# A planned instruction order for attention with a gated feed-forward block: planned again with four other times, and a last value product over 128 rows

## The chip, the cores and the metric

The kernel runs on one core of one Trainium2 chip. The metric is the device time of one execution in microseconds, the median of three runs. Beside it stands one execution that the hardware profiler recorded, with its own time; all rows of the profile come from that one.

## What is computed

Two branches on 2,048 tokens of width 512, mixed by a gate per token. The first is attention with 32 heads of 16 columns, the second a feed-forward block of width 1,376 whose hidden values are the product of two projections:

```python
g = sigmoid((x * gate_w).sum(-1))
q, k, v = split(x @ wqkv)              # 32 heads, 16 columns each
p = softmax(q @ k.T * 16 ** -0.5)
a = (p @ v) @ wo
b = ((x @ w_gate) * (x @ w_up)) @ w_down
out = g * a + (1 - g) * b
```

The feed-forward block is fed the same x. All inputs and the output are bf16.

## The kernel before, in words

**Tiles.** The tokens of the queries go in four chunks (c) of 512. A step is one of 32 groups of four heads for one chunk (a "quad", `quad`) and 128 keys (kt): four score blocks of 128 keys by 512 queries, one per head, then their exponentials, then the value products that add into bank 7 of PSUM. A matmul uses 64 rows and 32 columns of TensorE (PE), an eighth of it. Four matmuls side by side in the columns make a *job* (`pe64`, L1721); a job belongs to one of two row halves, r = 0 or 1, and both halves run jobs at the same time. Two score jobs of the same keys in a row share their weights, and the second leaves the weight load out (`keep`).

**Two ways for an exponential.** Steps of kind A go to ScalarE (ACT, `exp`, L1840). Steps of kind D go to VectorE (DVE, `dpass`, L1873), which makes a rough exponential by integer arithmetic; three more versions with other offsets are made by DVE or GpSimd (POOL, `copy`, L1879 and L1880), and all four are multiplied with the values. So a D step has eight value jobs, an A step two, one per half.

**Fill units.** Projections, the feed-forward products and the output products are units of 8 to 30 jobs (`_Unit`). They start strictly in the order of one list, `self.fill`, by `f_start` (L664): only the unit at its head may start, and only if what it reads is there.

**The planner.** No order is written out. `_Sched` (L138) simulates the engines event by event when the program is built, with a duration for every kind of instruction, and each decision appends an instruction to its engine's list. `_Plan.emit` then puts the lists out with semaphores for the true dependences. The chip follows the lists in order on each engine, and starts an instruction as soon as its semaphores allow; the planner's times are in no instruction. What decides between ready jobs are about 45 tables in `PAR` (limits of score blocks in flight, priorities, pairings). A table holds one entry per 2.0 us (`win`) of the planner's clock, written as (count, value) runs and read by `g` (L178); beyond its end the last entry is used. Before the change each table has 322 entries.

**Times that the planner assumes**, and that the change touches:

- `ilat`, in `take` (L262): instructions of PE come in packets of 256; a packet asked for near the end of the one before is taken to be there `ilat` later.
- `wgap`, in `weights` (L501), `late` (L507) and `wd_go` (L532): spacing of the weight loads on SP's queue. `weights` issues 36 loads: four pieces of w_up, four of w_gate, and so on in turn, then four of wo; a load is taken to land 3.0 us after its issue.
- `tx`, in `prologue` (L1508): when the four chunks of x, transposed by DMA (issued at L2048), are there.
- `mmarg`, in `norm2` (L1270): how long after the broadcast of the softmax denominators' reciprocals (rb, 256 KB, L2030) landed the multiplication of a normalized group is put on DVE (`mult`, L2038). POOL's copies wait for the last such multiplication.

**The end.** The last value product of quad 31 leads to `tail_norm` (L1986 to L1992: shuffle, product, logarithm and exponential for the reciprocal, product), and then to `tail_out` (L2001 to L2018): one more product of 128 rows for each of four output tiles, the sums with the feed-forward part, and the stores. The output products of the last chunk ("fin" units) run at the same time as the last value products.

`v_job` (L416) emits a value job and `pv` (L1771) its matmuls. A change of half in bank 7 waits for the last job of the other half.

Of the kernel before, what the change touches and what calls it, by code (L numbers as in the profile page):

```python
# [137 lines left out]
class _Sched:  # L138
# [277 lines left out]
    def v_job(self, r):  # L416
# [1141 lines left out]
    def run(self):  # L1558
# [22 lines left out]
        self.vcount = [0] * NG  # L1581
        self.vh = 0
# [72 lines left out]
class _Hw:  # L1655
# [385 lines left out]
    def prologue(self):  # L2041
# [114 lines left out]
        if self.par["acc"]:  # L2156
# [23 lines left out]
 'alook': ((3, 2), (1, 1), (5, 2), (16, 1), (2, 6), (25, 2), (4, 6), (1, 5), (1, 2), (2, 6), (9, 2), (1, 4), (1, 5),  # L2180
# [12 lines left out]
 'amax': ((4, 5), (5, 4), (3, 5), (1, 4), (4, 5), (2, 4), (2, 6), (1, 5), (2, 6), (21, 4), (1, 6), (6, 4), (5, 3),  # L2193
# [3 lines left out]
 'amin': ((3, 4), (1, 2), (12, 4), (1, 3), (4, 4), (1, 3), (5, 4), (10, 2), (1, 4), (1, 2), (6, 4), (1, 3), (4, 4),  # L2197
# [5 lines left out]
 'apick': ((16, 1), (3, 0), (3, 1), (5, 0), (3, 1), (5, 0), (4, 1), (3, 0), (3, 1), (1, 0), (4, 1), (2, 0), (5, 1),  # L2203
# [4 lines left out]
 'ares': ((7, 2), (2, 1), (4, 0), (8, 1), (1, 2), (16, 1), (1, 0), (1, 1), (5, 0), (2, 1), (3, 0), (2, 2), (3, 1),  # L2208
# [6 lines left out]
 'await': ((1, 0.1), (3, 0), (3, 0.2), (2, 0.05), (3, 0), (4, 0.05), (13, 0), (9, 0.05), (1, 0.1), (8, 0.05), (5, 0),  # L2215
# [168 lines left out]
 'lg': [3, 4],  # L2384
 'mga': 0.0,
 'mgd': 0.0,
 'mmarg': 0.6,
 'ndum': 6,
 'npre': 0,
 'olead': 2.2,  # L2390
# [145 lines left out]
```

## Time and profile before

| what | value |
|---|---|
| median of three runs | 654.78 us (654.52 to 656.81) |
| the profiled execution | 654.76 us |
| its span, first to last instruction | 653.0 us |
| matmuls, weight loads | 22,841 and 18,026 |
| granted clock of TensorE | 0.999 |

In rows by time, the first number is the start in us, the second the length; "x4" means four instructions merged. In rows of a group, three durations are the shortest, median and longest in ns, then come the first and last start. In rows of waits, the numbers are us in total, times, and (where there are three) the longest. In rows of a stretch, each engine's busy time stands with its count of instructions in brackets: PE, weight loads (PEld), DVE, ACT, POOL, then the granted clock, the share of the DMA engines and GB/s.

### The profile page before, as it was taken

The numbers are of one execution on the slowest core, as the hardware profiler recorded it, in microseconds if no ns is written. First come the engines' busy times: TensorE is split into PE (matmuls) and PEld (weight loads), VectorE is DVE, ScalarE is ACT, GpSimd is POOL, SyncE is SP. The second block draws the span as 40 slices with busy tenths as digits, with TensorE's granted clock in tenths as the row PEclk, the third lists the DMA queues.
The fourth block names the chain that finished last, engine by engine and source line by source line (L and its number), as shares of the span: only waits on it lengthen the run. The fifth ranks groups of instructions, "written<-read, shape, count | busy, mean of one in ns | idle before, by whom it ended". The sixth has DMA issues, their size and how long they took to land.

```text
span 653.0 us, 44030 instructions
## 1 busy us (share of the span) xinstructions
PE 645.0 (99%) x22841; PEld 337.8 (52%) x18026; DVE 608.5 (93%) x1001; ACT 639.6 (98%) x1001; POOL 535.0 (82%) x590
## 2 busy tenths in 40 slices
PE   8999999999999999999999999999999999999997
PEld 4564555555555545545554555545554554545552
DVE  7889999999999899999999999999999879999995
ACT  6999999999999999999999999999999999999995
POOL 1235889898999678899999798999998977997971
PEclk9999999999999999999999999999999999999999
DMA  7302341002110100101001010100101011010101
GB/s 155 77 13 61 89 110 36 9 11 70 52 45 6 38 29 17 34 6 38 5 20 32 18 40 13 36 15 14 28 8 43 13 31 37 5 44 8 30 11 45
DMA packets 34584, 22.66 MB, mean 35 GB/s; under 512 B 20028, under 2 KB 31132, under 8 KB 34400
## 3 DMA queue, kind: packets, MB, share of 16 engines
q1 hardware_dynamic: 32912, 18.80, 11.4%
q8 instruction: 160, 2.62, 1.7%
q10 hardware_dynamic: 1488, 1.05, 0.6%
q14 instruction: 24, 0.20, 0.1%
HBM read 11.71 MB, written 2.36 MB: 22 GB/s over the span
## 4 chain that ended last, share of the span: by engine, by line
PE 89%; ACT 5%; SPq 3%; POOL 1%; DMA 1%; DVE 0%; issue 0%; POOLq 0%
PE ps L1743 71%; PE ps L1728 18%; ACT wd L1840 3%; SPq L2048 3%; ACT PT L1840 2%; DMA xT<-in_A_x_dram 1%; POOL DB L1880 0%; DVE DB L1873 0%; POOL wk L1880 0%; POOLq L88 0%; POOL wq L1975 0%; ACT oc L2010 0%; DVE KT L1888 0%; PE ps L2001 0%; POOLq L83 0%
## 5 line engine op out<-in xcount | busy, mean ns | idle before, releaser
L1743 PE MATMUL ps<-QM,KT 64*32 64x512 bf16 x6956 | 490.5, 377 | 1.0 <-DVE QM L2148 0.6
L1880 POOL INT64_ADD DB<-DB x433 | 399.7, 940 | 78.2 <-DVE DB L1873 32.7
L1840 ACT ACTIVATE PT<-ps 128x512 bf16<-128x512 f32 (+1 forms) x660 | 443.1, 816 | 0.5 <-PE ps L1743 0.2
L1873 DVE TENSOR_SCALAR DB<-ps 128x512 int16<-128x512 f32 (+1 forms) x623 | 404.5, 684 | 25.5 <-PE ps L1743 21.2
L1743 PEld LDWEIGHTS ps<-QM,KT 64*32 64x32 bf16 x6956 | 158.0, 90 | 181.8 <-DVE DB L1873 49.9
L1728 PE MATMUL ps<-DB,Vp 64*17 64x512 bf16 x3092 | 239.9, 376 | 0.0
L1743 PE MATMUL ps<-PT,Vp 64*17 64x512 bf16 x1798 | 201.7, 376 | 0.0
L1743 PE MATMUL ps<-DB,Vp 64*17 64x512 bf16 x1924 | 182.5, 376 | 0.0
L1728 PE MATMUL ps<-QM,KT 64*32 64x512 bf16 x1236 | 118.5, 376 | 0.1
L1743 PE MATMUL ps<-xT,wu 64*32 64x512 bf16 x1376 | 114.0, 376 | 0.0
L1840 ACT ACTIVATE xT<-ps 128x512 bf16<-128x512 f32 (+1 forms) x144 | 113.0, 860 | 0.0
L1743 PE MATMUL ps<-xT,wg 64*32 64x512 bf16 x1376 | 111.0, 376 | 0.0
L1743 PE MATMUL ps<-xT,Vp 64*17 64x512 bf16 x432 | 84.8, 376 | 0.0
L1743 PE MATMUL ps<-wd,hT 64*32 64x512 bf16 x1152 | 84.7, 376 | 0.0
L1840 ACT ACTIVATE wd<-ps 128x512 bf16<-128x512 f32 (+1 forms) x123 | 70.8, 704 | 0.3
L1743 PEld LDWEIGHTS ps<-PT,Vp 64*17 64x17 bf16 x1798 | 55.7, 87 | 18.4 <-issue 5.1
L1743 PEld LDWEIGHTS ps<-DB,Vp 64*17 64x17 bf16 x1924 | 46.2, 86 | 21.3 <-issue 1.7
L1880 POOL INT64_ADD DB<-wv x50 | 43.4, 885 | 7.4 <-DVE wv L1873 4.1
L1873 DVE TENSOR_SCALAR wv<-ps 128x512 int16<-128x512 f32 (+1 forms) x63 | 42.3, 692 | 1.8 <-PE ps L1743 1.3
L1743 PEld LDWEIGHTS ps<-xT,wg 64*32 64x32 bf16 x1376 | 34.3, 91 | 16.4 <-issue 2.2
L1743 PEld LDWEIGHTS ps<-xT,wu 64*32 64x32 bf16 x1376 | 34.0, 91 | 17.1 <-issue 2.0
L1880 POOL INT64_ADD wv<-DB x32 | 31.6, 988 | 9.1 <-DVE OT L2038 3.0
(112 smaller groups left out, 744.8 us busy)
## 6 DMA issues: line engine op xcount, KB each, us to landing
rb<-rscr SPq DMA_DIRECT2D x16, 256.0 KB
QM<-qraw SPq DMA_DIRECT2D x120, 16.0 KB, 2.3
oc<-oraw SPq DMA_DIRECT2D x60, 32.0 KB, 2.2
out_dram<-ost SPq DMA_DIRECT2D x12, 128.0 KB, 1.8
wd<-in_B_w_down_dram SPq DMA_DIRECT2D x10, 128.0 KB, 2.3
wu<-in_B_w_up_dram SPq DMA_DIRECT2D x12, 96.0 KB, 2.5
wg<-in_B_w_gate_dram SPq DMA_DIRECT2D x12, 96.0 KB, 2.3
wv<-in_A_wqkv_dram ACTq DMA_DIRECT2D x1, 512.0 KB, 4.2
```

Source lines behind the costliest of these rows:

```text
L1728: o = pe.add_instruction(mybir.InstMatmult(name=nc.get_next_instruction_name(), engine=mybir.EngineType.PE, ins=[pe.lower_ap(rhs), pe.lowe ...
L1743: o = pe.matmul(dst, lhs, rhs, start=st, stop=sp, tile_position=(64 * r, 32 * cc), skip_group_check=True)
L1840: return self.P.op("act", lambda a: a.activation(dst, src, ACT.Exp, scale=self.ES), deps)
L1873: return self.dve(lambda v: v.tensor_scalar(dst, src, self.YB, 0.0, ALU.add, ALU.max), deps)
L1880: return self.P.op("pool", lambda e: e.int64_add(o.bitcast(I64), a.bitcast(I64), 0x0001000100010001 * self.OFF[v]), deps)
L2048: return P.dma(eng, lambda e: e.dma_start(dst, src, **kw), deps, stream)
```

## The change

Four times that the planner assumes are changed. All tables of `PAR` that choose between ready jobs are replaced by others, with 324 entries each, so that most instructions stand elsewhere in their engine's list. And the last value product of quad 31, if it is of kind A, is emitted once over all 128 rows in place of one job per half; it waits for the last value jobs of both halves. Constants of the planner that are not shown, durations included, stay.

```diff
@@ in v_job
-        if self.hw:
+        whole = False
+        if e.q == self.NG - 1:
+            whole = e.kind == "A" and self.vcount[e.q] == 15 and not first and (e in self.vfull or self.vj[0] == self.vj[1])
+            if not whole:
+                self.vj[r] += 1
+        if whole and self.hw:
+            if e in self.vfull:
+                op = self.vfull[e]
+            else:
+                c, b, s = self.quad(e.q)
+                old = [] if self.vfull else list(self.vl)
+                op = self.vfull[e] = self.hw.pv_whole(b, s, e.kt, self.pcells(e, v), list(ops) + self.dep([("v", e.kt)]) + old)
+        elif self.hw:
@@ new, beside pv
+    def pv_whole(self, b, s, kt, cells, deps):
+        def fn(pe):
+            o = None
+            for cc in range(4):
+                w = self.Vp[:, kt, 8 * b + 2 * cc + s, 0:17]
+                o = pe.matmul(self.ps[32 * cc : 32 * cc + 17, 7, :], w, self.cell(cells[cc], 0, 128), start=False, stop=True, tile_position=(0, 32 * cc), skip_group_check=True)
+            return o
+
+        return self.P.op("pe", fn, deps, "pex")
@@ in PAR
- 'ilat': 3.9,
+ 'ilat': 4.0,
- 'mmarg': 0.6,
+ 'mmarg': 1.6,
- 'tx': [6.4, 12, 16.5, 20.5],
+ 'tx': [6.4, 12, 16.5, 22.2],
- 'wgap': 1.2,
+ 'wgap': 2.0,
...
```

Of the tables, two are named later: `pp` lets a half issue the second job of a pair of score jobs at once (its entry is 1 in 123 of 322 before and in 171 of 324 after), and `vpp` does the same for value jobs of one D step (237 of 322 and 257 of 324).

More of the change, by code (lines that the diff above doesn't have):

```diff
@@ L1581, in run @@
         self.vcount = [0] * NG
+        self.vfull, self.vj = {}, [0, 0]
         self.vh = 0
@@ new lines @@
+ 'amax': ((2, 5), (10, 4), (5, 5), (5, 6), (5, 5), (22, 4), (3, 3), (6, 4), (2, 6), (4, 4), (1, 6), (13, 4), (1, 5),
+          (4, 4), (1, 5), (7, 4), (6, 6), (12, 4), (3, 6), (33, 4), (2, 3), (37, 4), (10, 5), (12, 4), (3, 3),
+          (42, 4), (2, 5), (14, 4), (1, 5), (16, 4), (3, 6), (1, 4), (11, 6), (2, 5), (10, 4), (3, 6), (1, 4), (3, 5),
+          (6, 6)),
+ 'amin': ((16, 4), (1, 3), (1, 2), (1, 4), (1, 2), (3, 4), (2, 3), (1, 4), (1, 2), (6, 4), (1, 3), (3, 2), (15, 4),
[4 rows of a table added]
+ 'apick': ((16, 1), (2, 0), (4, 1), (2, 0), (1, 1), (12, 0), (1, 1), (8, 0), (1, 1), (5, 0), (1, 1), (10, 0), (6, 1),
[3 rows of a table added]
@@ new lines @@
+ 'ares': ((12, 2), (4, 0), (1, 1), (1, 0), (1, 2), (3, 1), (1, 2), (2, 1), (2, 2), (6, 1), (4, 2), (15, 1), (1, 2),
[4 rows of a table added]
+ 'await': ((1, 0.1), (8, 0), (3, 0.05), (15, 0), (16, 0.05), (3, 0.2), (1, 0.05), (2, 0), (3, 0.1), (1, 0), (7, 0.05),
[10 rows of a table added]
+ 'cpmax': ((16, 18), (1, 8), (5, 18), (1, 14), (2, 8), (2, 24), (5, 4), (1, 14), (1, 18), (3, 4), (18, 14), (1, 10),
[6 rows of a table added]
+ 'dact': ((1, 1), (11, 4), (5, 3), (4, 1), (2, 4), (1, 3), (1, 4), (5, 3), (3, 4), (1, 3), (4, 4), (14, 2), (1, 3),
[4 rows of a table added]
+ 'dahead': ((22, 0), (1, 2), (2, 0), (21, 1), (9, 0), (1, 1), (2, 0), (2, 1), (9, 2), (1, 1), (1, 0), (5, 1), (3, 0),
[3 rows of a table added]
@@ new lines @@
+ 'dend': ((12, 3), (7, 1), (3, 5), (1, 2), (2, 1), (2, 4), (1, 1), (1, 0), (23, 1), (1, 3), (5, 1), (2, 2), (5, 0),
[5 rows of a table added]
+ 'dks': [1, 3, 5, 7, 9, 11, 13, 15],
[6 rows of a table added]
+ 'dlook': ((1, 2), (11, 0), (15, 1), (6, 2), (1, 1), (3, 2), (4, 1), (11, 2), (127, 1), (2, 2), (10, 1), (3, 2),
[7 rows of a table added]
+ 'dmaq': 2.0,
+ 'dmax': ((2, 3), (10, 2), (10, 1), (1, 4), (2, 1), (2, 3), (8, 2), (2, 4), (18, 2), (1, 4), (4, 2), (4, 4), (1, 2),
[4 rows of a table added]
+ 'dpair': ((1, 1), (15, 0), (1, 1), (6, 0), (2, 2), (2, 3), (6, 2), (1, 3), (3, 1), (5, 0), (3, 1), (1, 0), (2, 1),
[5 rows of a table added]
@@ L2317 @@
+ 'dpri': ((1, 1), (12, 0), (1, 1), (14, 0), (1, 1), (12, 0), (5, 1), (6, 0), (45, 1), (12, 0), (3, 1), (1, 0), (5, 1),
[3 rows of a table added]
+ 'dresv': ((2, 1), (8, 0), (2, 1), (1, 2), (1, 1), (3, 2), (5, 1), (1, 2), (2, 1), (2, 3), (3, 0), (4, 1), (4, 0),
[5 rows of a table added]
+ 'dwait': ((2, 0.4), (15, 0.2), (1, 0), (1, 0.2), (1, 0), (2, 0.2), (1, 0.4), (2, 0.2), (2, 0), (7, 0.1), (3, 0),
[6 rows of a table added]
+ 'fcf': ((12, 1), (312, 0)),
+ 'fdebt': ((1, 25), (11, -10), (1, 10), (1, -10), (2, -30), (6, 10), (1, 0), (10, 10), (1, 25), (3, -30), (4, -10),
[3 rows of a table added]
  'ffn0': 2.6,
@@ L2329 @@
- 'fres': ((315, 0), (2, 2), (2, 0), (1, 1), (2, 0)),
- 'fs2': ((11, 1), (1, 0), (12, 1), (4, 0), (3, 1), (4, 0), (3, 1), (1, 0), (21, 1), (1, 0), (9, 1), (2, 0), (7, 1),
-         (9, 0), (217, 1), (4, 0), (1, 1), (7, 0), (5, 1)),
- 'fstart': ((1, 2), (3, 1), (23, 2), (2, 1), (2, 2), (4, 1), (3, 2), (1, 1), (33, 2), (3, 1), (1, 2), (17, 1),
[3 rows of a table removed]
+ 'flead': ((9, 10), (3, 20), (5, 0), (1, 20), (1, 0), (3, 20), (3, 0), (2, 40), (1, 20), (1, 0), (4, 20), (1, 0),
[5 rows of a table added]
+ 'fmax': ((7, 3), (5, 2), (11, 3), (2, 2), (5, 3), (4, 2), (50, 3), (1, 2), (8, 3), (4, 2), (11, 3), (19, 2), (2, 3),
+          (8, 2), (26, 3), (5, 2), (11, 3), (15, 2), (20, 3), (5, 2), (53, 3), (1, 2), (31, 3), (4, 2), (1, 3),
+          (2, 1), (7, 3), (1, 1), (2, 3), (2, 2), (1, 3)),
@@ new lines @@
+ 'fres': ((101, 0), (4, 1), (206, 0), (3, 1), (1, 0), (3, 2), (1, 1), (5, 0)),
+ 'fs2': ((5, 1), (4, 0), (16, 1), (9, 0), (16, 1), (2, 0), (31, 1), (2, 0), (1, 1), (7, 0), (2, 1), (2, 0), (178, 1),
+         (4, 0), (7, 1), (1, 0), (24, 1), (3, 0), (1, 1), (3, 0), (6, 1)),
+ 'fstart': ((3, 2), (2, 1), (3, 2), (4, 1), (1, 2), (1, 1), (9, 2), (4, 1), (2, 2), (4, 1), (37, 2), (2, 1), (1, 2),
+            (13, 1), (3, 2), (4, 1), (6, 2), (28, 1), (2, 2), (23, 1), (8, 2), (2, 1), (1, 2), (4, 1), (14, 2),
+            (19, 1), (27, 2), (8, 1), (28, 2), (7, 1), (9, 2), (6, 1), (2, 2), (1, 1), (20, 2), (1, 1), (6, 2),
+            (3, 1), (6, 2)),
@@ L2424 @@
  'rmarg': 0.3,
[L2425 removed]
[5 rows of a table removed]
[L2431 removed]
[6 rows of a table removed]
+ 'skew': ((6, 2), (2, 3), (2, 6), (2, 4), (2, 6), (2, 4), (1, 2), (13, 6), (3, 4), (25, 6), (1, 3), (1, 2), (44, 6),
[3 rows of a table added]
+ 'skewd': ((1, 1), (15, 2), (1, 3), (5, 2), (1, 3), (4, 2), (2, 3), (4, 4), (1, 2), (3, 4), (9, 1), (2, 4), (5, 2),
[6 rows of a table added]
  'sp0': 17.0,
@@ L2440 @@
  'tw': [(('wk', False), 0), (('wq', False), 0), (('wv',), 10.5), (('gw',), 18.0)],
[1 row of a table removed]
[1 row of a table added]
  'ugdur': 1.131,
[3 rows of a table removed]
- 'vgrp': ((24, 2), (3, 0), (1, 2), (7, 0), (6, 2), (2, 0), (2, 2), (1, 4), (1, 2), (4, 0), (1, 4), (5, 3), (1, 2),
[4 rows of a table removed]
- 'vpp': ((12, 0), (1, 1), (3, 0), (3, 1), (2, 0), (1, 1), (2, 0), (48, 1), (4, 0), (3, 1), (8, 0), (1, 1), (11, 0),
-         (2, 1), (1, 0), (41, 1), (3, 0), (13, 1), (4, 0), (33, 1), (2, 0), (1, 1), (4, 0), (4, 1), (2, 0), (2, 1),
-         (1, 0), (1, 1), (13, 0), (5, 1), (2, 0), (10, 1), (5, 0), (65, 1), (4, 0), (3, 1), (2, 0)),
- 'vpre': ((1, 1), (3, 0), (1, 2), (14, 0), (5, 2), (3, 1), (1, 0), (3, 1), (4, 0), (3, 4), (1, 0), (3, 4), (3, 0),
[5 rows of a table removed]
- 'vpref': ((6, 0), (1, 2), (2, 3), (1, 1), (2, 3), (1, 0), (4, 1), (2, 0), (2, 1), (1, 3), (2, 0), (3, 2), (9, 1),
[7 rows of a table removed]
[3 rows of a table added]
+ 'vgrp': ((1, 3), (13, 2), (2, 4), (11, 2), (9, 0), (1, 4), (9, 0), (7, 2), (2, 0), (1, 2), (2, 0), (2, 4), (2, 2),
[4 rows of a table added]
+ 'vpp': ((16, 0), (2, 1), (1, 0), (3, 1), (1, 0), (50, 1), (6, 0), (5, 1), (1, 0), (6, 1), (2, 0), (39, 1), (21, 0),
+         (6, 1), (3, 0), (67, 1), (5, 0), (20, 1), (1, 0), (58, 1), (1, 0), (1, 1), (9, 0)),
+ 'vpre': ((1, 1), (18, 0), (4, 4), (2, 0), (2, 1), (10, 4), (23, 0), (5, 4), (2, 1), (2, 4), (3, 2), (1, 4), (6, 1),
[4 rows of a table added]
+ 'vpref': ((1, 0), (1, 1), (10, 0), (2, 2), (9, 1), (2, 3), (2, 1), (7, 2), (4, 3), (1, 1), (13, 0), (1, 2), (3, 0),
[5 rows of a table added]
  'warmto': 0.0,
- 'wgap': 1.2,
+ 'wgap': 2.0,
  'win': 2.0,
[15 rows of a table removed]
[11 rows of a table added]
  'xq': 0,
```

37 lines of the change are left out of this document (6 added, 31 removed), and 408 rows, old and new, of the table PAR.

## Prediction

> **What bounds the kernel now.** I read the page first, then busy time in stretches, the matrix engine's order of time, the waits and the transfers. The profiled execution took 654.76 us, 1.76 more than its span; the median of the runs is 654.78, so sums made against the one hold for the other.
>
> ```profile
> span 653.0 us, 44030 instructions
> PE 645.0 (99%) x22841; PEld 337.8 (52%) x18026; DVE 608.5 (93%) x1001; ACT 639.6 (98%) x1001; POOL 535.0 (82%) x590
> PE 89%; ACT 5%; SPq 3%; POOL 1%; DMA 1%; DVE 0%; issue 0%; POOLq 0%
> ```
>
> PE and ACT are both busy nearly all the time, and the chain that ended last lies on PE for 89%. But a busy PE need not be full: a matmul of 64 rows by 32 columns uses an eighth of the array. Three consecutive jobs of one row half show the pace, and the stretches show where PE stood still:
>
> ```profile
> 21.54 0.39 PE L1743 MATMUL ps<-wv,xT 64*32 64x512 bf16 x4
> 22.85 0.40 PE L1743 MATMUL ps<-xT,wk 64*32 64x512 bf16 x4 [0.93 <-DMA xT<-in_A_x_dram]
> 23.07 0.40 PE L1743 MATMUL ps<-xT,wk 64*32 64x512 bf16 x4
> 23.28 0.40 PE L1743 MATMUL ps<-xT,wk 64*32 64x512 bf16 x4
> ...
> 8.40:21.50 13.10, 12.42 (x401) 6.20 (x356) 10.98 (x18) 13.09 (x22) 2.24 (x3) 1.00 0.63 123
> 21.50:22.90 1.40, 0.47 (x24) 0.08 (x14) 1.21 (x2) 0.97 (x2) 0.00 (x0) 1.00 0.46 111
> 22.90:153.80 130.90, 130.85 (x4764) 69.81 (x3748) 124.33 (x204) 129.92 (x238) 99.29 (x103) 1.00 0.20 50
> 153.80:154.60 0.80, 0.49 (x24) 0.07 (x16) 0.80 (x3) 0.80 (x3) 0.74 (x1) 1.00 0.08 21
> 154.60:584.50 429.90, 429.90 (x15405) 224.01 (x12173) 407.42 (x656) 429.49 (x643) 384.97 (x422) 1.00 0.10 27
> 584.50:585.00 0.50, 0.43 (x20) 0.12 (x11) 0.21 (x1) 0.50 (x1) 0.50 (x2) 1.00 0.17 41
> 585.00:647.50 62.50, 62.50 (x2200) 32.65 (x1690) 56.14 (x96) 60.67 (x92) 45.27 (x55) 1.00 0.06 17
> ```
>
> A job (four matmuls) starts every 0.215 us in each half. 57 of the 22,841 matmuls belong to the prologue and the very end; the other 22,784 make 5,696 jobs of four, 2,848 in each half: 612 us of the 639 between 8.5 and 647.5. So 27 us of half slots are unused. In contrast, PE stands still altogether for 0.68 + 0.93 + 0.05 + 0.31 + 0.07 = 2.0 us in that stretch. This is the first thing to see: **there is little waiting to remove**; what the time depends on is how tightly the planned order packs the two halves while ACT and DVE keep up.
>
> **The change part by part.** None of the four new planner values adds a wait to the program. They are beliefs by which the planner sorts; on the chip an instruction still goes as soon as its semaphores allow. A value can therefore gain only what a wrong belief cost, and may lose by what a timid one forbids.
>
> *Later x (20.5 to 22.2).* The last x tiles are needed by the K projection of the last 512 tokens:
>
> ```profile
> 18.32 4.39 DMA xT<-in_A_x_dram
> ```
>
> They land at 22.71; the planner had the projection at the head of PE's queue before that. PE's starts go from 21.54 to 22.85, 1.31 us instead of 0.215: 1.1 us lost. Behind this one load were V projections, scores and value products, all ready. Sorted after 22.2 on the planner's clock, they run first. I take -1.1; ends 0 (other work isn't ready then) and -1.3 (the whole gap).
>
> *Later multiplications (0.6 to 1.6).* Each of the 16 waits on DVE for the broadcast reciprocals:
>
> ```profile
> L2038 DVE TENSOR_TENSOR OT<-oc,rb x16: 679/682/1139, 76.5 to 640.0; 128x512 bf16<-128x512 f32 x16
>   DMA rb<-rscr: 0.3, 1
>   POOL DB L1880: 9.5, 11
>   POOL wv L1880: 3.0, 3
> 642.41 0.39 PE L1743 MATMUL ps<-wo,OT 64*32 64x512 bf16 x4
> ```
>
> Once in 16 DVE waited, 0.3 us; queued behind it were score passes, for which PE waits. POOL's 12.5 us behind these multiplications stay, since its copies are tied to them. Placed 1.0 later, the last ends at 640.0 + 1.0 + 0.7 = 641.7, 0.7 before the first output product of the last chunk at 642.41: hidden, and without that cover it would cost up to 1.0. The gain is counted below with the other small stalls.
>
> *Spaced weight loads (1.2 to 2.0).* SP issues them one after the other already; the value moves their place among SP's transfers and the time at which the planner believes them landed.
>
> ```profile
> 57.09 2.02 SPq L1964 DMA_DIRECT2D wu<-in_B_w_up_dram  x4
> 59.15 2.94 SPq L1964 DMA_DIRECT2D wg<-in_B_w_gate_dram  x4
> L1743 PE MATMUL ps<-xT,wu x1376: 373/376/388, 62.4 to 595.3; 64*32 64x512 bf16 x197
> L1743 PE MATMUL ps<-xT,wg x1376: 373/376/388, 66.7 to 598.5; 64*32 64x512 bf16 x197
> L1743 PE MATMUL ps<-wo,OT x480: 376/376/388, 207.5 to 646.9; 64*32 64x512 bf16 x160
> ```
>
> The first wg group would be believed complete seven spacings after the first wu load, 57.1 + 14.0 + 3.0 = 74.1 instead of 68.5, so the first gate unit (66.7 here) moves by 5.6 to 7.4 us. The units of the fill list start strictly in its order, so a Q and four K projections queue behind it; scores, value products and running units are the cover. Two units are 16 jobs, 16 x 0.215 / 2 = 1.7 us of PE: cost between 0 and 1.7, contained in the order's length below. The last of these 36 loads, for wo, would be believed landed at 57.1 + 35 x 2.0 + 3.0 = 130.1; wo is first read at 207.5, so it is covered.
>
> *Later packets (3.9 to 4.0).*
>
> ```profile
> q8 instruction: 160, 2.62, 1.7%
> PEld ps L1743 <- issue: 20.0, 80, 0.5
> 32.00:48.00 16.00, 16.00 (x600) 9.76 (x476) 14.02 (x24) 16.00 (x31) 6.48 (x8) 1.00 0.06 14
> ...
> 0.00:16.00 16.00, 13.84 (x262) 7.71 (x246) 11.62 (x34) 11.04 (x17) 2.85 (x9) 1.00 0.79 157
> 640.00:656.00 16.00, 8.49 (x235) 3.28 (x188) 6.14 (x15) 6.42 (x9) 1.45 (x2) 0.91 0.11 35
> ```
>
> 160 packets of 16 KB bring 22,841 + 18,026 instructions, 256 each. No full stop of PE in the stream is put down to issue; the weight loads' 20.0 us in pieces of at most 0.5 lie beside matmuls of the other half. I take 0 on the chip, between 0 and -2.0 (all full stops). The page "Runtime: NRT & Kernel Launch" of the Trainium skill, section "Instruction fetch mechanics", says that the sequencer fetches the next 256 instructions while it executes the current ones, so that a boundary is mostly hidden; the rows agree. By that rule the sum has 0 here; by the opposite, each of 159 packets 0.1 late, up to -16.
>
> *Last value product over 128 rows.* It replaces two jobs, one after the other in the two halves, by four matmuls:
>
> ```profile
> 644.69 0.39 PE L1743 MATMUL ps<-PT,Vp 64*17 64x512 bf16 x4
> 644.91 0.38 PE L1743 MATMUL ps<-PT,Vp 64*17 64x512 bf16 x2
> 645.36 0.45 DVE L1986 STREAM_SHUFFLE rb<-ps 128x256 f32<-128x256 f32 x1
> 647.13 0.39 PE L1743 MATMUL ps<-wq,OT 64*32 64x512 bf16 x4
> 647.68 0.98 PE L2001 MATMUL ps<-wq,OT 128*128 128x512 bf16 x3 [0.16 <-issue]
> ```
>
> The final chain on DVE and ACT could start one to two slots earlier, 0.2 to 0.45 us; the change of shape costs something, as from 64*32 to 128*128 at 647.13, where 0.55 passes between starts instead of 0.215. I take -0.2, ends -0.45 and +0.35. "TensorEngine Tiling (Array Packing)" of the Trainium skill, section "Key Properties", says that changing the tiling mode drains the engine; here it would happen twice, since output products in 64 rows follow. Counted by the row just named that is 2 x 0.33 = +0.7 against -0.45, +0.25 in all: no result of its own.
>
> *The order itself.* All but a few of the planner's tables are new, so most instructions move, and no row of before shows the new sequence. One size can be read off the source: a table entry stands for 2.0 us of the planner's clock, and each table has 322 entries before and 324 after. That is a length, not a measured time, but the trace calibrates it: the old tables end between 642 and 644, and the last planned job started at 647.13, so the chip ran 3.1 to 5.1 (4.1) behind the clock. x accounts for 1.1 of that; 3.0 are smaller stalls, such as this one, 0.69 between starts:
>
> ```profile
> 153.84 0.39 PE L1728 MATMUL ps<-DB,Vp 64*17 64x512 bf16 x4
> 154.53 0.40 PE L1743 MATMUL ps<-QM,KT 64*32 64x512 bf16 x4 [0.30 <-ACT PT L1840]
> ```
>
> The new tables end between 646 and 648: +4.0 with bounds +2.0 and +6.0. From this go the 1.1 of x and, since later multiplications, loads and packets are now believed, half of the 3.0: -1.5, bounds 0 and -3.0.
>
> Sum: +4.0 - 1.1 - 1.5 - 0.2 = +1.2, **656.0 us**.
>
> **Rivals.**
>
> *The new stalls equal the old (slower).* Small stalls come from chance meetings of transfers, POOL copies and DVE in the order, and a new order has new ones. Place: DVE's queue, where one late instruction holds score passes and then PE, as at 153.8. Against it: the cautious values. If the stalls take back the 1.5 and the end saves nothing, 654.8 + 4.0 - 1.1 = 657.7; if x waits as well, 658.8. This is also the case in which the change doesn't do what it says. It passes 0.5% when the lag stays above 3.6 us.
>
> *Packets pace the plan (slower).* In 32 to 48 there are 1,076 instructions, 4.2 packets; at 4.0 us these fill 16.8. Over the 41 rows of this table, whose first and last are quoted, 29 exceed 1,024 instructions, by 13.7 us in all; about 15 per row are counted twice at the edges, which leaves 7. If the new plan stretches them, 654.8 + 7 - 1.1 = 660.7. It decides only if pairs of jobs that share a weight load don't become more frequent; against it, table pp allows pairs in 171 of 324 entries instead of 123 of 322, vpp in 257 instead of 237.
>
> *Only the stalls go (faster).* If the last two entries are never reached and the order is as tight as before, the gain is 1.1 + 3.0 + 0.2 = 4.3: 650.5. It needs the lengths to be an accident; the old ones fit their trace.
>
> **How the numbers follow.** Forecast 656.0: chance 0.71, its own range 652.5 to 658.0. Lag unchanged: 0.13; half of that lies above 658.0. Packets: 0.07. Only the stalls: 0.09. A measurement of this kernel can tell about 0.5%, 3.3 us, from no change. Faster 0.08 (nearly all of the last case), slower 0.17 (the packets, half of the lag case, and 0.03 of the forecast's tail where its bounds +6.0 and 0 meet), same 0.75. The range 651.8 to 659.6 reaches to the lag case whole and leaves out most of the two outer cases.
>
> **What would show it.** Right: no wait on xT near 22; the first K projection of the last tokens after 22.7; PE's full stops below 1 us between 8.5 and 648; the last planned job near 648.5; fewer weight loads than 18,026 and 159 packets or less; a group of 128*32 matmuls near the end. Wrong: the last planned job before 645 (the tables' length meant nothing), a stop of over 1 us at another place (the lag moved), or waits on issue well over 20 us.

## The result, and the profile after

The changed kernel takes 657.07 us (median, 654.96 to 659.66), the kernel before, on the same chip, 655.26 (653.97 to 656.81): a ratio of 1.0027 with a 95% interval of 1.0017 to 1.0037. That is 1.8 us, a slowdown that is clear of zero but stays within the 0.5% named in the prediction. The profiled execution took 657.00 us, 1.8 more than its span.

From the page of the changed kernel: the span, the busy time of each engine, the instruction queue, and the shares of the chain that ended last.

```profile
span 655.2 us, 43615 instructions
PE 646.8 (99%) x22814; PEld 333.9 (51%) x17622; DVE 604.6 (92%) x989; ACT 642.3 (98%) x1008; POOL 541.4 (83%) x599
q8 instruction: 158, 2.59, 1.7%
PE 96%; DVE 2%; DMA 1%; ACT 0%; issue 0%; POOLq 0%; SPq 0%
```

404 weight loads, two packets and 27 matmuls fewer (mostly one D step that became an A step, and the product over 128 rows), and still 2.2 us more span: PE has less to do and takes longer over it. The stretches of the changed kernel, with its own full stops cut out, say where it stood (columns as before: length, PE, weight loads, DVE, ACT, POOL, clock, DMA share, GB/s):

```profile
8.40:21.50 13.10, 12.26 (x400) 6.19 (x340) 11.42 (x19) 13.06 (x18) 6.81 (x10) 1.00 0.70 122
21.50:22.90 1.40, 1.40 (x56) 0.61 (x40) 1.17 (x3) 1.40 (x3) 0.00 (x0) 1.00 0.42 84
22.90:73.20 50.30, 50.30 (x1792) 26.62 (x1376) 44.03 (x72) 50.22 (x87) 27.66 (x33) 1.00 0.18 47
73.20:74.50 1.30, 0.48 (x28) 0.06 (x9) 1.30 (x3) 1.30 (x4) 1.30 (x2) 1.00 0.87 221
74.50:157.30 82.80, 82.69 (x3016) 45.13 (x2275) 78.79 (x129) 81.85 (x144) 74.43 (x97) 1.00 0.20 47
157.30:158.80 1.50, 0.99 (x42) 0.27 (x25) 1.09 (x2) 1.50 (x4) 1.35 (x3) 1.00 0.00 0
158.80:584.50 425.70, 425.63 (x15221) 218.51 (x11788) 401.67 (x644) 424.79 (x645) 381.47 (x403) 1.00 0.10 27
```

In 21.50 to 22.90 PE started 56 matmuls where it started 24 before: the x stop is gone. At 73.20 to 74.50 it did nothing for 0.82 us, in a stretch where nothing stood before. And in the long stretch the pace itself is a little lower: 15,221 matmuls in 425.7 us are 35.75 per us, before 15,405 in 429.9 were 35.83; over 430 us that is 0.9 us.

The projection of the last x tiles, and the other half beside it, in the order of time of the changed kernel (no releaser stands behind the rows):

```profile
23.02 0.39 PE L1756 MATMUL ps<-wv,xT 64*32 64x512 bf16 x4
23.09 0.39 PE L1741 MATMUL ps<-QM,KT 64*32 64x512 bf16 x4
23.24 0.39 PE L1756 MATMUL ps<-wv,xT 64*32 64x512 bf16 x4
23.41 0.40 PE L1756 MATMUL ps<-xT,wk 64*32 64x512 bf16 x4
```

The new stop at 73.3, on PE, then on SP's queue, then the group of gate units:

```profile
73.27 0.38 PE L1756 MATMUL ps<-wd,Vp 64*17 64x512 bf16 x3
74.47 0.40 PE L1756 MATMUL ps<-xT,wg 64*32 64x512 bf16 x4 [0.81 <-DVE DB L1896]
74.48 0.40 PE L1756 MATMUL ps<-xT,wq 64*32 64x512 bf16 x4
```

```profile
56.02 1.81 SPq L1987 DMA_DIRECT2D wu<-in_B_w_up_dram  x4
62.74 0.60 SPq L1966 DMA_DIRECT2D den<-oraw  x1
63.39 2.93 SPq L1971 DMA_DIRECT2D oc<-oraw  x4
66.36 1.20 SPq L2058 DMA_DIRECT2D rscr<-rec  x2
67.60 2.02 SPq L1987 DMA_DIRECT2D wg<-in_B_w_gate_dram  x2
69.66 0.65 SPq L2053 DMA_DIRECT2D rb<-rscr  x1
70.36 0.93 SPq L1987 DMA_DIRECT2D wg<-in_B_w_gate_dram  x2
```

```profile
L1756 PE MATMUL ps<-xT,wg x1376: 372/376/387, 74.5 to 600.7; 64*32 64x512 bf16 x197
```

PE's starts go from 73.27 to 74.47, 1.20 us. The releaser that the row names is DVE; but the job is the first that reads w_gate, and by its semaphore the last of the four pieces landed at 74.33, 0.14 us before the job. Before, the four pieces of w_gate were issued as one run at 59.15, right behind those of w_up. Now 7.2 us of other transfers' issues lie between, and the last two pieces stand behind the 256 KB broadcast of reciprocals at 69.66; the DMA engines are at 0.87 in the stretch.

The stop at 157.5, again in the order of time, PE and its weight loads:

```profile
157.46 0.38 PE L1756 MATMUL ps<-PT,Vp 64*17 64x512 bf16 x1
158.35 0.38 PE L1756 MATMUL ps<-PT,Vp 64*17 64x512 bf16 x1 [0.51 <-issue]
```

```profile
158.35 0.08 PEld L1756 LDWEIGHTS ps<-PT,Vp 64*17 64x17 bf16 x1 [1.01 <-issue]
```

It cuts one job of four matmuls in two: the fourth had not come with its packet. Two packets in a row lie 5.5 us apart here; the median gap is 4.0. The place says the same: counted from the start, the late instruction is number 9,410 of PE's matmuls and weight loads, that is 36 x 256 + 194, and 69 of the 72 long stops of a_nokeep, below, lie 193 or 194 past a multiple of 256. The stop at 153.84 of the kernel before, which the prediction put on DVE's queue, has the number 9,410 too: by its place it was a late packet.

The end, in the order of time:

```profile
646.68 0.38 PE L1756 MATMUL ps<-xT,Vp 64*17 64x512 bf16 x2
647.13 0.39 PE L1798 MATMUL ps<-xT,Vp 128*17 128x512 bf16 x2
647.14 0.39 PE L1798 MATMUL ps<-PT,Vp 128*17 128x512 bf16 x2
647.46 0.41 PE L1756 MATMUL ps<-wo,OT 64*32 64x512 bf16 x8
...
649.67 0.45 PE L1756 MATMUL ps<-wq,OT 64*32 64x512 bf16 x8
```

The value product over 128 rows is there, with a gap of 0.45 us ahead of it and 0.32 behind it where 0.215 is the pace. The 0.45 is a wait that the change puts there: the product waits for the last value jobs of both halves, and the last of them ended at 647.06. Behind the 0.32 the trace shows no wait.

Adding up, for the profiled executions, how far the starts of consecutive matmuls lie apart beyond 0.23 us, from 12 to 646 us: 2.53 us before (1.07 of it the x stop), 2.75 after (0.97 at 73.3, 0.66 at 157.5). The stops did not become less; they changed places. Most of the others belong to the order: the same ones, of 0.3 to 0.5 us and at the same instructions, are in the other traces of the old order too (near 71, 113, 428, 491 and 584 us), and another set in those of the new (near 115, 352 and 507). The planned stream, from the first planned matmul to the last of the kernel, took 648.28 - 8.47 = 639.8 us before and 650.71 - 8.17 = 642.5 after: 2.7 us longer, 0.2 of it stops, and 2.5 the order itself and what these stops leave out.

One pair of executions is little for this. From the first planned matmul to the last planned job, with every stop beyond 0.23 us taken out, five traces of the old order (the kernel before, b_whole, b_xpiece, b_xpiece2, b_smallrb) take 635.0, 636.3, 635.3, 636.1 and 634.8 us, four of the new (the changed kernel, a_wgfirst, a_nowhole, a_smallrb) 636.9, 637.2, 636.7 and 636.9. The pair above gives 1.9 in this way, since the stops before 12 us and at the end are out too; the means give 1.4. The planner says where this comes from. `_Sched` can be run by itself, without a chip: it starts the first job at 7.60 us of its clock in both kernels and the last at 642.70 before and 644.86 after. The new order was planned 2.2 us longer.

### The profile page after: what moved, and what is told of

Its sections match the earlier page's. It is cut to its first block, busy times and chain, and to the rows that moved or that the text cites. A ratio compares the mean times of both kernels' runs of the same rounds, so it can differ in the third digit from the quotient of the medians.

```text
span 655.2 us, 43615 instructions
## 1 busy us (share of the span) xinstructions
PE 646.8 (99%) x22814; PEld 333.9 (51%) x17622; DVE 604.6 (92%) x989; ACT 642.3 (98%) x1008; POOL 541.4 (83%) x599
## 4 chain that ended last, share of the span: by engine, by line
PE 96%; DVE 2%; DMA 1%; ACT 0%; issue 0%; POOLq 0%; SPq 0%
PE ps L1756 75%; PE ps L1741 20%; DVE DB L1896 1%; DMA wq<-in_A_wqkv_dram 1%; ACT wu L1863 0%; PE ps L2151 0%; DVE wv L1896 0%; POOLq L88 0%; DVE usb L1930 0%; DVE KT L1911 0%; SPq L2071 0%; ACT oc L2033 0%; DVE hT L1937 0%; DVE qraw L1914 0%; DVE oraw L1961 0%
## 5 line engine op out<-in xcount | busy, mean ns | idle before, releaser
L1756 PE MATMUL ps<-QM,KT 64*32 64x512 bf16 x6668 | 489.4, 377 | 0.8 <-ACT wu L1863 0.8
L1863 ACT ACTIVATE PT<-ps 128x512 bf16<-128x512 f32 (+1 forms) x694 | 459.2, 810 | 0.9 <-PE ps L1756 0.5
L1896 DVE TENSOR_SCALAR DB<-ps 128x512 int16<-128x512 f32 x618 | 403.6, 686 | 27.6 <-PE ps L1756 22.2
L1756 PEld LDWEIGHTS ps<-QM,KT 64*32 64x32 bf16 x6668 | 154.2, 90 | 182.3 <-DVE DB L1896 48.0
L1741 PE MATMUL ps<-DB,Vp 64*17 64x512 bf16 x3188 | 239.9, 376 | 0.0
L1756 PE MATMUL ps<-PT,Vp 64*17 64x512 bf16 x1854 | 206.3, 376 | 0.5 <-issue 0.5
L1756 PE MATMUL ps<-DB,Vp 64*17 64x512 bf16 x1788 | 172.0, 376 | 0.1
L1741 PE MATMUL ps<-QM,KT 64*32 64x512 bf16 x1524 | 148.0, 376 | 0.1
L1863 ACT ACTIVATE xT<-ps 128x512 bf16<-128x512 f32 (+1 forms) x147 | 113.8, 865 | 0.1
L1756 PE MATMUL ps<-xT,Vp 64*17 64x512 bf16 x424 | 81.5, 376 | 0.0
L1756 PEld LDWEIGHTS ps<-PT,Vp 64*17 64x17 bf16 x1854 | 56.5, 86 | 21.2 <-issue 7.2
L1863 ACT ACTIVATE wd<-ps 128x512 bf16<-128x512 f32 (+1 forms) x105 | 63.0, 700 | 0.9 <-PE ps L1756 0.9
L1896 DVE TENSOR_SCALAR wv<-ps 128x512 int16<-128x512 f32 x60 | 39.5, 683 | 1.0 <-PE ps L1756 0.7
L1903 POOL INT64_ADD wk<-DB x36 | 36.8, 1024 | 2.7 <-DVE DB L1896 2.0
```

Source lines behind the costliest of these rows:

```text
L1741: o = pe.add_instruction(mybir.InstMatmult(name=nc.get_next_instruction_name(), engine=mybir.EngineType.PE, ins=[pe.lower_ap(rhs), pe.lowe ...
L1756: o = pe.matmul(dst, lhs, rhs, start=st, stop=sp, tile_position=(64 * r, 32 * cc), skip_group_check=True)
L1863: return self.P.op("act", lambda a: a.activation(dst, src, ACT.Exp, scale=self.ES), deps)
L1896: return self.dve(lambda v: v.tensor_scalar(dst, src, self.YB, 0.0, ALU.add, ALU.max), deps)
L1903: return self.P.op("pool", lambda e: e.int64_add(o.bitcast(I64), a.bitcast(I64), 0x0001000100010001 * self.OFF[v]), deps)
```

## The experiments

Each was timed in rounds with the kernel before on the same chip, and the ratios are to that kernel. For orientation, all of them:

| kernel | median, us | ratio to before, 95% interval |
|---|---|---|
| changed kernel | 657.07 | 1.0027 (1.0017 to 1.0037) |
| a_wgfirst | 655.83 | 1.0012 (1.0002 to 1.0022) |
| a_nowhole | 657.04 | 1.0027 (1.0013 to 1.0041) |
| a_smallrb | 656.41 | 1.0013 (0.9999 to 1.0027) |
| a_keep34 | 657.44 | 1.0040 (1.0025 to 1.0055) |
| a_nokeep | 691.85 | 1.0578 (1.0549 to 1.0608) |
| b_whole | 655.48 | 1.0002 (0.9989 to 1.0014) |
| b_klater | 656.33 | 1.0014 (1.0003 to 1.0026) |
| b_kl8_2 | 657.40 | 1.0031 (1.0014 to 1.0049) |
| b_xpiece | 654.40 | 0.9987 (0.9973 to 1.0001) |
| b_xpiece2 | 655.38 | 0.9995 (0.9983 to 1.0007) |
| b_smallrb | 654.68 | 0.9993 (0.9982 to 1.0004) |
| b_ilat | 706.81 | 1.0787 (1.0757 to 1.0818) |

Names with a_ are edits of the changed kernel, names with b_ of the kernel before.

My theory after the result: the order is about 2 us longer than the old one, the x stop is gone, and the late load of w_gate takes its place. The rivals: the value product over 128 rows costs the 2 us through its two gaps; or late packets and the broadcasts ahead of them do; or the x wait was worth nothing in the first place.

### The load of w_gate ahead of the other transfers (a_wgfirst)

```diff
+        ops = hw.P.ops
+        mv = [o for o in ops if o.stream == "dwg0"]
+        ops[:] = [o for o in ops if o.stream != "dwg0"]
+        at = max(i for i, o in enumerate(ops) if o.stream == "dwu0") + 1
+        ops[at:at] = mv
...
         hw.P.emit(nc, stack)
```

> The changed kernel with the first four w_gate loads moved ahead on SP's list, straight behind the first four w_up loads and so ahead of the denominators, the copies and the 256 KB broadcast of the reciprocals; every other list is the same. Theory (the wait on x was exchanged for a wait on w_gate): PE's stop of 1.19 us between starts near 73.3 goes, and the time falls by 0.8 to 1.2 us, so from about 1.8 above the kernel before to about 0.8 above it. Rival (the stop is covered, the time is lost in the order as a whole): the stop goes and the time stays within 0.3 us.

Measured: 655.83 us. SP's queue of this kernel, then its PE at the place of the stop:

```profile
56.69 2.48 SPq L1987 DMA_DIRECT2D wu<-in_B_w_up_dram  x4
59.21 1.85 SPq L1987 DMA_DIRECT2D wg<-in_B_w_gate_dram  x4
```

```profile
73.92 0.38 PE L1756 MATMUL ps<-wd,Vp 64*17 64x512 bf16 x3
73.95 0.39 PE L1756 MATMUL ps<-xT,wg 64*32 64x512 bf16 x4
```

Nothing but the place of four loads differs, and the first gate job follows at the pace. The medians differ by 1.24 us, the ratios by 0.0015, which is 1.0 us; the two intervals overlap a little. The releaser in the trace of the changed kernel was the wrong one: w_gate it was. The load's landing shows it in every trace. Its last piece landed at 74.33 in the changed kernel, 73.82 in a_nowhole and 75.39 in a_keep34; the first gate job starts 0.14 us later in each, after 1.19, 0.52 and 1.43 us between starts. Here it had landed at 63.84, and there is no stop. So the price of the stop varies from execution to execution, around 1 us. (In the trace of a_keep34, below, the waits name the load itself.)

### Without the value product over 128 rows, and with it in the old order (a_nowhole, b_whole)

```diff
-            whole = e.kind == "A" and self.vcount[e.q] == 15 and not first and (e in self.vfull or self.vj[0] == self.vj[1])
+            whole = False and e.kind == "A" and self.vcount[e.q] == 15 and not first and (e in self.vfull or self.vj[0] == self.vj[1])
```

> The changed kernel with the last value product as two jobs of 64 rows again, nothing else. By the prediction's sum: 0.2 us slower than the changed kernel, so some 2.0 above the kernel before. If the change of shape costs more than it saves: 0.2 to 0.7 faster than the changed kernel.

Measured: 657.04 us beside 657.07. The end of its trace goes straight on:

```profile
646.13 0.38 PE L1756 MATMUL ps<-PT,Vp 64*17 64x512 bf16 x2
646.31 0.42 PE L1756 MATMUL ps<-wo,OT 64*32 64x512 bf16 x8
```

The rival that these two gaps cost 2 us falls. With intervals of 0.7 and 0.9 us to each side, a difference of 0.2 us can't be told from none. b_whole takes the code of the change (`v_job` and `pv_whole`) into the kernel before, with the old values and tables.

> The kernel before with the last value product over 128 rows and nothing else of the change. By the prediction's sum: 0.2 us faster, between 0.45 faster and 0.35 slower. Rival (the change of shape makes PE run empty twice): 0.2 to 0.7 slower, with gaps of over 0.3 us between matmul starts on both sides of the 128*32 group.

Measured: 655.48 us, 1.0002. It tells nothing of the product: no group of 128*17 is in its trace, since the old order does not end the quad in a way that meets the condition. It is the kernel before once more, and shows how well the comparison returns 1.

### The K projection of the last tokens later, by hand (b_klater, b_kl8_2)

In the kernel before, the jobs of the unit that waited for x (`mv`, those of unit `("k", 0, 3)`) are moved down PE's list; b_kl8_2 also moves the copy of their result in VectorE's list.

```diff
+        for o in reversed(mv):
+            k = pe.index(o)
+            pe.remove(o)
+            k += 10
...
+            pe.insert(k, o)
```

> The kernel before with the eight jobs of the K projection of the last 512 tokens ten places later on PE's list, behind scores and V projections that are ready; all other lists keep their order. Theory (the x wait is a pure loss): PE's stop of 1.31 us between starts at 21.5 shrinks to under 0.5 and the time falls by 0.8 to 1.2 us against the kernel before. Rival (the jobs pulled ahead fill the gap, but VectorE and ScalarE, which were idle there too, are what is late afterwards): the stop goes and the time falls by less than 0.4 us.

Measured: 656.33 us, slower by 1.2. VectorE's list, then PE's, in this kernel:

```profile
26.89 0.69 DVE L1892 CAST KT<-ps 128x512 bf16<-128x512 f32 x1 [1.90 <-PE ps L1746]
```

```profile
26.67 0.39 PE L1746 MATMUL ps<-QM,KT 64*32 64x512 bf16 x4
27.64 0.40 PE L1746 MATMUL ps<-wv,xT 64*32 64x512 bf16 x4 [0.58 <-DVE KT L1892]
```

PE no longer waits for x, but DVE now stands 1.90 us in front of a copy whose input comes later, and PE stands behind DVE: the V unit in the row reads nothing of that copy, so what it waits for is the PSUM bank that the copy empties. So DVE's list was moved too, with PE's by eight places instead of ten:

```diff
+            k += 8
...
+        e = next(o for o in dv if any(d in mv for d in o.deps))
+        k = dv.index(e)
+        dv.remove(e)
+        dv.insert(k + 2, e)
```

> The kernel before, with the jobs of the K projection of the last tokens put eight places later in TensorE's list and VectorE's copy of their result two places later in VectorE's; every other list is unchanged. Theory (a stall goes for good only where every engine's list gives way): the wait on xT at 21.5 us, 1.30 us of full stop, goes, VectorE does not stand as it did for 1.90 us at 26.9 in the run with TensorE's list alone changed, and the time falls by 0.5 to 1.1 us, to about 654.0 to 654.6 beside 655.1. Rival one: the list after it runs as late as it did, held by VectorE or ScalarE, and the time stays within 0.3 us. Rival two: as with TensorE's list alone, about 1 us slower, with a new stop near 27 us.

Measured: 657.40 us, slower by 1.9; the theory's number failed and rival two was nearer. In its order of time:

```profile
27.24 0.39 PE L1746 MATMUL ps<-QM,KT 64*32 64x512 bf16 x4
28.97 0.40 PE L1746 MATMUL ps<-wv,xT 64*32 64x512 bf16 x4 [1.34 <-DVE KT L1892]
```

The later copy lets go of its PSUM bank later, and the V unit that takes this bank next stands 1.73 us between starts, longer than the stop that was to be removed. (In this trace the last load of x landed at 20.94, so that there was no stop for x to remove; the next section has more on this.) A job that is put later at one place of a packed order makes wait what hangs on it: DVE's copy, and the bank behind the copy.

### The same wait, cut in four (b_xpiece, b_xpiece2)

Every list stays; each of the first half's four jobs waits for the one load that it reads.

```diff
+            if u.name == ("k", 0, 3) and u.ph == 0:
+                xp = self.hw.r["xp"]
+                deps = [d for d in deps if d not in xp] + [xp[i]]
...
-..., "dxt%d" % ch, transpose=True)
+..., "dxt%d" % (ch if ch < 3 else 3 + kt), transpose=True)
```

> The kernel before, every list in its order; only the wait of the first half of the K projection of the last tokens is cut in four: each of its four jobs waits for the one of the four transposing loads that it reads, in place of all four jobs waiting for the last. Theory (the stop is worth what it lasts, as long as no list gives another in its place): three jobs pass before the last load has landed, 0.65 of the 1.30 us of full stop at 21.5 go, VectorE's and ScalarE's lists have nothing new to wait for, and the time falls by 0.4 to 0.8 us, to about 654.4 to 654.9 beside 655.3. Rival (the lists behind the stop take its time up again, at VectorE or at a PSUM slot, as when the jobs were moved): within 0.2 us, or slower.

Measured: 654.40 us, with an interval that reaches 1.0001. In its trace the jobs do go one by one:

```profile
20.71 0.40 PE L1746 MATMUL ps<-xT,wk 64*32 64x512 bf16 x4
21.86 0.40 PE L1746 MATMUL ps<-xT,wk 64*32 64x512 bf16 x4 [0.73 <-DMA xT<-in_A_x_dram]
22.75 0.40 PE L1746 MATMUL ps<-xT,wk 64*32 64x512 bf16 x4 [0.49 <-DMA xT<-in_A_x_dram]
```

and the last is 0.75 us earlier than before (23.50). But the stops are longer in sum than the one of 1.30, since in this execution the planned stream began at 7.33 instead of 8.47 while the last load of x landed at 22.71 in both. A second series:

> The kernel before with the wait on the transposing loads cut in four, once more, since the interval of its first run reached from 0.9973 to 1.0001. Theory: 0.4 to 0.8 us faster again, the first half of the K projection of the last tokens through at 22.75 in place of 23.50 us. Rival: the first ratio was chance, within 0.2 us.

Measured: 655.38 us, ratio 0.9995. In that trace nothing waits for x at all: the four jobs start at 21.95, 22.16, 22.38 and 22.60, and the last load of x had landed at 20.88, before the first of them. The gain of 0.4 to 0.8 us is not shown; the two ratios together lie at about 0.999, and both intervals hold 1.

So the x stop is not in every execution. Over the 14 profiled executions of this study the last load of x landed between 22.7 and 23.2 in eight, between 20.5 and 21.2 in five, and at 21.87 in b_smallrb, where PE's stop was 0.71 instead of 1.30; the first planned matmul started between 7.3 and 8.6. What the stop lasts is the difference between a landing and a start that both vary. Why the load comes early or late stays open. The changed kernel's order starts the unit at 23.4 in either case (x landed at 22.96 in its own trace, at 20.54 in that of a_nowhole): so it avoids the stop where x is late, and where x is early there is none to avoid.

### The broadcast cut to an eighth (b_smallrb, a_smallrb)

```diff
-        src = bass.AP(c.tensor, c.offset, [[512, 8], [0, 16], [1, 512]])
+        src = bass.AP(c.tensor, c.offset, [[512, 8], [0, 16], [1, 64]])
...
```

> The kernel before, with the broadcast of the reciprocals to rb cut from 512 columns to the first 64 for each row (32 KB in place of 256 KB); the other columns of rb hold 1.0 from the start, so seven eighths of the output's normalization is left out. Theory (late packets come behind these broadcasts): fewer gaps over 4.7 us between the packets of TensorE, the stops of TensorE near 113.8, 153.8 and 584.5 us (0.42, 0.68 and 0.45 us) go, and the time falls by 0.5 to 1.5 us. Rival: the late packets are chance and have nothing to do with the broadcast: as many stops as before, at other places, and the time within 0.3 us.

> The changed kernel with the same cut of the broadcast to 64 of 512 columns (seven eighths of the normalization is left out). Theory (late packets behind the broadcasts): the stops near 115.0 and 157.5 us (0.49 and 0.89 us) go, the time falls by 0.5 to 1.5 us from 657.07, and the stop at 73.3 us (1.19 us), which comes from the load of w_gate, stays or shrinks to about 0.8 since a broadcast stands ahead of that load on SP's list. Rival: the broadcast costs nothing; within 0.3 us of 657.07.

Measured: 654.68 and 656.41 us. By the ratios the first is 0.5 us below the kernel before, in an interval that holds no difference, the second 0.9 below the changed kernel, with intervals that overlap. The stops tell more than the times. In a_smallrb the late packet is still there (0.69 at 156.4, instruction 9,410 again), so the theory on the packets falls: late packets come without large broadcasts too. The stops near 113 and 584 that I had laid to packets stay in both kernels where they were (0.42 and 0.45 in b_smallrb, 0.52 at 113.8 in a_smallrb); they are the order's own. The one of 153.8 is missing in the trace of b_smallrb, as it is in those of b_whole and b_xpiece2, which have the whole broadcast. The stop at 73.3, which I expected to shrink to 0.8, is gone altogether. SP's queue of a_smallrb:

```profile
67.58 0.93 SPq L1987 DMA_DIRECT2D wg<-in_B_w_gate_dram  x2
68.80 0.65 SPq L2053 DMA_DIRECT2D rb<-rscr  x1
69.50 0.93 SPq L1987 DMA_DIRECT2D wg<-in_B_w_gate_dram  x2
```

The loads of w_gate keep their place behind the broadcast here, are issued 0.86 us earlier, and have 32 KB instead of 256 KB ahead of them. The last piece landed at 71.97, 2.0 us after its issue; behind the 256 KB it took 3.5 in the changed kernel, 3.0 in a_nowhole and 5.0 in a_keep34. By these traces it is the broadcast ahead that makes the load late. Both kernels without this stop lie at 1.0012 and 1.0013; but since b_smallrb fell by 0.5 us without any such stop, the time of a_smallrb proves less than its trace.

### Weight loads and packets (a_nokeep, a_keep34)

```diff
-                if keep:
+                if False:
```

> The changed kernel, every list in its order, with each matrix product loading its weights, also those that find theirs already loaded: 22,814 loads in place of 17,622. Theory (loads of weights lie beside running products, so their number by itself decides nothing and the 404 loads that the change saves brought nothing): 0 to 1 us slower. Rival (a load is on TensorE's path): the 5,192 loads more, at 18.9 ns each (333.9 us over 17,622), would give up to 98 us, and the 404 that the change saves would be worth up to 7.6 us, which would then have hidden a loss of that size elsewhere.

Measured: 691.85 us, 34.8 slower: my theory fell, and by far. The page and the waits on PE of this kernel:

```profile
PE 668.6 (97%) x22813; PEld 388.9 (57%) x22814; DVE 608.7 (88%) x989; ACT 656.0 (95%) x1008; POOL 540.9 (79%) x599
q8 instruction: 178, 2.92, 1.8%
```

```profile
PE ps L1756 <- issue: 9.2, 30, 0.9
```

and one of 72 stops over 0.3 us (67 of them before 646 us) in its order of time:

```profile
446.86 0.38 PE L1756 MATMUL ps<-xT,wu 64*32 64x512 bf16 x3
448.11 0.37 PE L1756 MATMUL ps<-xT,wu 64*32 64x512 bf16 x1 [0.86 <-issue]
```

Again a job cut in two. 69 of the 72 stops lie 193 or 194 instructions past a multiple of 256, and these 69 hold 21.8 us beyond the pace: they are packet boundaries. Between stops the jobs go at 0.215 us. In that time both halves start 16 instructions, so a packet of 256 lasts 3.4 us, and PE stands until the next one is there; the median gap between packets is 3.73 us. In the changed kernel a packet brings more matmuls, lasts 4.0 us, and one of its stops is such a boundary. "Runtime: NRT & Kernel Launch" of the Trainium skill, section "Instruction fetch mechanics", calls the cost of crossing such a boundary mostly hidden; this run shows a limit of that for PE: where it used up a packet in 3.4 us, the packets came 3.73 us apart in the median. 20.5 of the 32.9 us of longer span are full stops beyond those of the changed kernel, by the same count from 12 us on; the other 12 I did not take apart. Is it the loads or the packets? A quarter of the loads tells:

```diff
+        if keep:
+            self.nkeep += 1
+            keep = self.nkeep % 4 != 0
```

> The changed kernel, every list in its order; of the jobs that find their weights already loaded every fourth loads them again (about 1,298 loads more, a quarter of those of the run in which all load). In that run TensorE stopped for 0.3 to 1.4 us in 67 places, 30 of them waits on issue, with one packet of 256 TensorE instructions each 3.73 us. Theory (a packet costs only where TensorE uses it up faster than the next comes): with a quarter of the loads a packet lasts about 3.95 us in the mean, against 4.0 in the changed kernel, and only the densest stretches stop; 0 to 3 us slower than 657.07. Rival (each load has its price, 34.8 us over 5,192): a quarter of 34.8, 8.7 us slower, to about 665.8.

Measured: 657.44 us, 0.4 above the changed kernel by the medians and 0.9 by the ratios, with 18,918 loads. Not 8.7, so a load has no fixed price: 1,296 loads more cost under 1 us, and 5,192 cost 34.8. Packets explain it: five stops over 0.3 us lie at boundaries here (0.34 to 0.64 us), one in the changed kernel, 69 in a_nokeep. Its waits on PE also name the load that the changed kernel's trace did not:

```profile
PE ps L1761 <- DMA wg<-in_B_w_gate_dram: 1.1, 1, 1.1
```

### One value alone (b_ilat)

```diff
- 'ilat': 3.9,
+ 'ilat': 4.0,
```

> The kernel before with one value alone of the change, the spacing of instruction packets in the plan, 3.9 to 4.0, with the due times and tables as they were. Theory (the values and the tables only fit one another): the planned order falls apart and comes out tens of us longer, 680 to 710 us. Rival (the value moves one packet by a little and the rest of the order holds): within 3 us of the kernel before.

Measured: 706.81 us. This value can't be judged by itself: with it moved by 0.1 and the old tables, the kernel is 51 us slower. The planner, run by itself with these values, puts the last job at 694.30 instead of 642.70: the order is long already as planned. Whether the other three values alone do as much was not tried.

## Why the prediction was right, and what in it was not

The time was 657.07 us beside 656.0 forecast, inside the range and inside "within 0.5%". As a difference to the kernel before on the same chip it was +1.8 beside +1.2. The steps fared less evenly.

- **x.** Right in the trace: no wait on xT, the first K projection of the last tokens at 23.41, after 22.7. The price of 1.1 was that of the profiled execution's stop; it is not the price of every execution, since the last load of x landed early in five of the 14 traces, and b_xpiece and b_xpiece2 don't show that the time falls by as much. And the way was more than I said: V projections, scores and value products "run first" only if DVE and the banks are planned again too, as b_klater and b_kl8_2 show.
- **Order length.** Right in sign, too large: +4.0 from two table entries, +1.9 in the pair of traces and +1.4 in the means. The tables' length was the wrong measure. They run to the last event of the planner's clock, and in the changed kernel that is the arrival of a packet behind all jobs, at 647.89, where the last job starts at 644.86; before, it is the end of the tail at 643.86, and the last job starts at 642.70. So of the 4.0 only 2.2 were jobs. The last planned job started at 649.67, not near 648.5 as I wrote: 4.8 us behind its planned time, beside 4.4 before (647.13), so the lag did not shrink. The lower pace over the long stretch accounts for 0.9 of the longer order; what in the tables makes it longer is not isolated by a run.
- **Half of the small stalls, -1.5.** This failed. Full stops went from 2.53 to 2.75 us. The 3.0 us that I called smaller stalls were a remainder, and my own stretches show only 1.1 us of full stops beside the one for x, and half of these is 0.6; the example at 153.84 was, by its place, a late packet. The new stop came from the loads, which I had priced in another place: the first gate unit moved from 66.7 to 74.5 us, a little more than the 5.6 to 7.4 that I gave, and I put its cost of 0 to 1.7 into the order's length. It was a stop of its own, of 1.0 to 1.2 us by a_wgfirst. I had seen that the spacing lets other transfers in between, and not that the planner takes a load to land 3.0 us after its issue even behind a broadcast of 256 KB. So the stop of over 1 us at another place, which I had named as a sign of being wrong ("the lag moved"), is there at 73.3: the mechanism of the first rival, at SP's queue instead of DVE's.
- **Multiplications.** No wait on rb is left, and the last multiplication ends before the output products of the last chunk, as worked out (it ends at 642.9, the first of them starts at 644.1). Nothing can be told of its price alone.
- **Packets.** 0 was right for this change: 158 packets, and one stop over 0.3 us at a packet boundary, as before. But my reading that the rows agree with a hidden boundary was too general: the stop of 0.68 at 153.84 was one that was not hidden, and a packet of the changed kernel lasts 4.0 us, only 7% more than the 3.73 at which packets came in a_nokeep.
- **The product over 128 rows.** -0.2 came out as no difference (a_nowhole), within intervals that could not show it. The gap of 0.45 us ahead of it is the wait for the value jobs, which I had not counted. The 0.32 behind it, 0.11 beyond the pace, has no wait in the trace. There the array changes its tiling mode, at which "TensorEngine Tiling (Array Packing)" of the Trainium skill, section "Key Properties", states a drain; no run here tells the drain from another cause.

The sum of what was measured, for the two profiled executions: +1.9 (order) - 1.1 (x stop) + 1.0 (w_gate) + 1.1 (other stops: 0.3 more at packet boundaries, 0.3 before 12 us, 0.5 in the last 3 us of the stream) - 0.7 (an earlier start and a shorter end) is +2.2, the difference of the spans; the medians differ by 1.8. Against my sum the order is 2.1 less, the stops are 3.6 more and the ends 0.5 less. That the forecast still came within 0.6 us of the measured difference is luck: two large errors hid each other.

No version beats both kernels with an interval that leaves out 1: the kernel before with the cut wait comes nearest (0.9987 and 0.9995), and the changed kernel with its load mended stays above the kernel before (1.0012).

## What to carry to other kernels

In an order planned to 99% of the bound engine, a wait is not worth its length: ask what next waits behind the thing that you let come later (the copy, then the bank), and whether the wait is there in every execution or only where a load happens to land late. The length of a planner's table is not the length of its plan: run the planner and look at its last job. When a plan spaces loads more widely, look at what then goes between them on the same queue; a large transfer ahead of the last piece is a new stop, and the profile may name the wrong releaser for it; the time at which the load landed settles it. A stop that recurs at the same instruction in every execution belongs to the order; one that comes and goes at a packet boundary does not. An instruction left out on a busy engine can be worth little for a while and decisive beyond a point: here what counted was how long a packet of 256 lasts.

## What the hardware showed that I had not expected

- In a_nokeep packets of 256 PE instructions came 3.73 us apart in the median while PE used one up in 3.4: it stopped for over 0.3 us at 69 packet boundaries, 21.8 us in all, and the kernel was 34.8 us slower. With a quarter of the added instructions it was 0.4 us.
- Single packets come late by 0.7 to 1.7 us (gaps of 4.7 to 5.7 us in the stream around a median of 4.0), with and without large broadcasts; one can stop PE for up to 0.9 us. The places differ between executions of the same list, though one boundary (instruction 9,410) is late in four traces, two of each order.
- The last transposed load of x landed at 20.5 to 21.2 us in five traces and at 22.7 to 23.2 in eight, of the 14. With the packets and a start that varies by up to 1.2 us this makes much of the spread of 3 to 5 us among the times of one kernel, I think; no run isolated it.
- Behind the product over 128 rows, with no wait in the trace, 0.32 us pass between starts in place of 0.215.
